# Multiplying w2 and the first 16 rows of wo in three TensorE loops with register addresses

## The chip, the cores and the metric

The kernel runs on one NeuronCore of a Trainium2 chip. The metric is the device time of one execution in microseconds. The core has five engines with instruction streams of their own: TensorE (PE; its weight loads are listed apart as PEld), VectorE (DVE), ScalarE (ACT), GpSimd (POOL) and SyncE (SP), which here only issues transfers. Each engine has a sequencer that reads the instructions, runs branches, register work and waits itself, and hands the rest to the engine. Data moves between HBM and the on-chip memory (SBUF, 128 partitions) through 16 DMA engines; TensorE writes its results to another memory, PSUM.

## What is computed

One decoded token `x` (1,024 values) is normalised, and two branches are added to it: attention with 32 query heads over the last 4,096 positions of a cache with 4 key/value heads, and a two-layer MLP.

```python
xn = _layernorm(x)
# A: attention over the last W = 4096 positions
q = xn @ wq                                   # 32 heads x 128
p = softmax(q . k / sqrt(128))                # k, v repeated 8 times
o = p . v                                     # 4096 values
A = o @ wo                                    # [4096] x [4096, 1024]
# B: MLP
h = gelu(layernorm(xn) @ w1 + b1)             # 3584 values
B = h @ w2 + b2                               # [3584] x [3584, 1024]
out = x + A + B
```

All tensors are bfloat16. Nearly all of the work is reading 39.9 MB: 4 MB each of K and V, and the matrices wq, w1, w2 and wo.

## The kernel before

With one token, every product is a vector times a matrix. The vector is the stationary operand of TensorE, one column of 128 values at a time, and the matrix streams through in pieces of 128 rows by 512 columns; the result is one row of 512 sums in PSUM. To use more of the array, such matmuls are placed in groups of columns of the array that start at 0, 32, 64 or 96 (`tile_position`); the output row then lies in the PSUM partition of the same number.

The stages follow each other so. The large transfers go through one queue that SP issues: K (L72), wq (L81), w1 (L207), V (L213), w2 (L221), wo (L229). They land in a ring of four tiles of 32 KB per partition, so a transfer waits until an older tile of the ring has been read. w2 comes in two tiles of 14 rows each, wo in two tiles of 16 rows; a "row" here is a piece of 128 matrix rows by 1,024 columns. The second wo tile is transferred in five parts, of 8, 4, 2, 1 and 1 rows, so that the last part to land is small.

Meanwhile VectorE and ScalarE transpose K (L186 to L202), TensorE forms q (L238) and the first MLP layer (L258), the scores (L276), the softmax follows, and TensorE multiplies the probabilities with V (L320). The first MLP layer's sums pass through the gelu on ScalarE (L313) and a transpose on VectorE (L315) into `hT`, whose column 32c holds the 128 values of h that belong to row c of w2. The attention result is brought into the same form as `o8` (L330 to L332), one column of 128 values per row of wo.

The last stage adds everything up in the PSUM tile `accf`, whose partitions 0 and 32 hold the two halves of the 1,024 outputs; x and b2 have been put there early (L178). A loop in the kernel's Python, unrolled into straight code (L339 to L342), goes over the 28 rows of w2 and 28 of the 32 rows of wo. Each row takes two matmuls, one for each half: the first in the column group at 0, the second in the group at 32. The last four rows of wo are the tail: their sums go to two other PSUM tiles, while ScalarE and VectorE copy `accf` out (L345, L346); the two parts are added (L353, L361, L362) and written to HBM.

POOL clears and fills small constants at the start, and computes the two reciprocal roots of the layer norms (L145, L168).

Of the kernel before, what the change touches and what calls it, by code (L numbers as in the profile page):

```python
# [9 lines left out]
BF16 = mybir.dt.bfloat16  # L10
# [6 lines left out]
def kernel(  # L17
# [14 lines left out]
    nc = tc.nc  # L32
    P = 128
    D = A_x.shape[-1]
# [12 lines left out]
    CW2 = Fd // P  # L47
    CWO = NQ // P
# [5 lines left out]
    consts = ctx.enter_context(tc.tile_pool(name="consts", bufs=1))  # L54
# [8 lines left out]
    def ring_tile(name):  # L63
        return ring.tile([P, RING_ELEMS], BF16, tag="ring", name=name, align_bytes=256)
# [13 lines left out]
    for i in range(2):  # L78
        t = ring_tile(f"wq{i}")
# [92 lines left out]
    accf = ps_acc.tile([P, 512], FP32, tag="accf")  # L172
# [3 lines left out]
    for half in range(2):  # L176
        pr = 32 * half
        nc.tensor.matmul(accf[pr:pr + 1, :], lhsT=ones_bf[0:2, 0:1], rhs=xb2[:, 512 * half:512 * half + 512],  # L178
                         start=True, stop=False, tile_position=(0, pr))
# [24 lines left out]
    for i in range(2):  # L204
        t = ring_tile(f"w1{i}")
# [6 lines left out]
        src = A_v_cache[0, g0:g1, Sk - W:Sk, :].rearrange("g (p c) d -> p g c d", p=P)  # L212
        nc.sync.dma_start(out=v4[:, g0:g1, :, :], in_=src)  # L213

    chunk_src = []
    w2_v = B_w2.rearrange("(p c) n -> p c n", p=P)
    for i in range(2):
        nr = CW2 // 2
        t = ring_tile(f"w2{i}")
        tv = t[:, :nr * D].rearrange("p (r n) -> p r n", r=nr)  # L220
        nc.sync.dma_start(out=tv, in_=w2_v[:, nr * i:nr * (i + 1), :])  # L221
        chunk_src += [("h", nr * i + r, tv[:, r, :]) for r in range(nr)]
    wo_v = A_wo.rearrange("(p c) n -> p c n", p=P)
    for i, cuts in enumerate([[0, 16], [0, 8, 12, 14, 15, 16]]):
        nr = CWO // 2
        t = ring_tile(f"wo{i}")
        tv = t[:].rearrange("p (r n) -> p r n", r=nr)
        for a, b in zip(cuts[:-1], cuts[1:]):
            nc.sync.dma_start(out=tv[:, a:b, :], in_=wo_v[:, nr * i + a:nr * i + b, :])  # L229
        chunk_src += [("o", nr * i + r, tv[:, r, :]) for r in range(nr)]  # L230


    for i, w3 in enumerate(wq_tiles):
        for r in range(4):
            c = 4 * i + r
            for j in range(NJQ):
                b, t = divmod(j, 4)
                nc.tensor.matmul(accq[32 * t:32 * t + 1, b, :], lhsT=xnT[:, c:c + 1], rhs=w3[:, r, j * 512:(j + 1) * 512],  # L238
                                 start=(c == 0), stop=(c == C - 1), tile_position=(0, 32 * t))
# [8 lines left out]
    for j in range(8):  # L248
        t, b = divmod(j, 2)
        nc.tensor.matmul(acch[32 * t:32 * t + 1, b, :NH], lhsT=ones_bf[0:1, 0:1], rhs=b1_row[:, j * NH:(j + 1) * NH],  # L250
                         start=True, stop=False, tile_position=(0, 32 * t))
    for i, w3 in enumerate(w1_tiles):
        for r in range(4):
            c = 4 * i + r
            for b in range(2):
                for t in range(4):
                    j = 2 * t + b
                    nc.tensor.matmul(acch[32 * t:32 * t + 1, b, :NH], lhsT=yT[:, c:c + 1], rhs=w3[:, r, j * NH:(j + 1) * NH],  # L258
                                     start=False, stop=(c == C - 1), tile_position=(0, 32 * t))
# [11 lines left out]
    for a in range(WQ4 // 512):  # L271
        sp = ps_f.tile([P, 512], FP32, tag="pf", name="sp")
        for R in range(4):
            for g in range(Hkv):
                c0 = WQ4 * R + 512 * a
                nc.tensor.matmul(sp[32 * R:32 * R + 32, :], lhsT=qm[:, g, :], rhs=kT[:, g, c0:c0 + 512],  # L276
                                 start=(g == 0), stop=(g == Hkv - 1), tile_position=(0, 32 * R))
# [31 lines left out]
    h_sb = consts.tile([P, 2 * NH], BF16)  # L309
    zcol = small.tile([P, 1], FP32, tag="zcol")  # L310
    nc.vector.tensor_scalar_mul(out=zcol[:], in0=l_loc[:], scalar1=0.0)  # L311
    for b in range(2):
        nc.scalar.activation(out=h_sb[:, b * NH:(b + 1) * NH], in_=acch[:, b, :NH], func=ACT.Gelu_apprx_tanh, bias=zcol[:])  # L313
    hT = consts.tile([P, CW2, 32], BF16)
    nc.vector.transpose(out=hT[:], in_=h_sb[:].rearrange("p (d c) -> p c d", c=CW2))  # L315


    o_all = ps_f.tile([Hq, Hkv, Dh], FP32, tag="pf", name="o_all")
    for c in range(NCH):
        nc.tensor.matmul(o_all[:].rearrange("h g d -> h (g d)"), lhsT=eTb[:, 32 * c:32 * c + 32], rhs=v4[:, :, c, :],  # L320
                         start=(c == 0), stop=(c == NCH - 1))
# [6 lines left out]
    o8_ps = ps_f.tile([P, 32], FP32, tag="pf", name="o8_ps")  # L328
    for q in range(4):
        nc.tensor.matmul(o8_ps[:], lhsT=spread[:, q, :], rhs=o_bf[:, 32 * q:32 * q + 32], start=(q == 0), stop=(q == 3))  # L330
    o8 = consts.tile([P, 32], BF16)
    nc.vector.tensor_copy(out=o8[:], in_=o8_ps[:])  # L332


    vec = {"h": lambda c: hT[:, c, 0:1], "o": lambda c: o8[:, c:c + 1]}
    N1 = 320
    TAIL = 4
    n_bulk = len(chunk_src) - TAIL
    for idx, (kind, c, wap) in enumerate(chunk_src[:n_bulk]):  # L339
        for half in range(2):  # L340
            nc.tensor.matmul(accf[32 * half:32 * half + 1, :], lhsT=vec[kind](c), rhs=wap[:, half * 512:(half + 1) * 512],  # L341
                             start=False, stop=(idx == n_bulk - 1), tile_position=(0, 32 * half))  # L342
# [7 lines left out]
    for idx, (kind, c, wap) in enumerate(chunk_src[n_bulk:]):  # L350
        if idx == TAIL - 2:
            for half in range(2):
                nc.tensor.matmul(acct[1][32 * half:32 * half + 1, :], lhsT=ident_f[0:33, 32 * half:32 * half + 1], rhs=bulk[1][:],  # L353
                                 start=False, stop=False, tile_position=(0, 32 * half))
        for t, (n0, n1) in zip(acct, cols):
            for half in range(2):
                nc.tensor.matmul(t[32 * half:32 * half + 1, :], lhsT=vec[kind](c),  # L357
                                 rhs=wap[:, half * 512 + n0:half * 512 + n1],
                                 start=(idx == 0), stop=(idx == TAIL - 1), tile_position=(0, 32 * half))
# [36 lines left out]
```

## Time and profile before

| | us |
|---|---|
| runs, median of 2 (101.69 to 102.08) | 101.88 |
| span of the profiled execution | 100.0 |
| median over the profiled span | 1.9 |
| PE busy / PEld busy | 51.2 / 20.0 |
| DVE busy / ACT busy / POOL busy | 49.7 / 34.1 / 3.8 |
| mean granted TensorE clock | 0.778 of full speed |
| read from HBM | 39.86 MB, 398 GB/s over the span |

The span runs from the first to the last instruction of one execution that the hardware profiler recorded; the 1.9 us beside it lie around the program. A busy time is the time in which an engine has at least one instruction under way. Waits, branches, register work and the issuing of transfers are not counted as busy. The granted clock is the share of TensorE's full clock that it was given, which changes during the run between 0.5 and 1. In all tables of the profile L12 is line 12 of the kernel, `out<-in` names the tiles, and "<-" behind an idle time names what ended it.

### The profile page before, as it was taken

Reading aid. Unit: us, or ns where it says so; the run is one execution under the profiler, and the core shown is the slowest. Engines: PE = TensorE matmul, PEld = TensorE weight load, DVE = VectorE, ACT = ScalarE, POOL = GpSimd, SP = SyncE. Lnnn points to the kernel's source line nnn. Section 1 sums busy time; section 2 is a strip of 40 time slices with the busy share of each in tenths; the row PEclk is TensorE's granted clock in tenths of the full one; section 3 lists DMA queues with packets and bytes.
Section 4 is the critical chain, followed back from the end, with each engine's and each line's share of the span. In section 5 each row is a group of like instructions: output and inputs, shape, how many; then the busy total and the mean of one; then the engine's idle time right before and its main releaser. Section 6 shows DMA issues by size and latency. Waiting matters only on the chain.

```text
span 100.0 us, 970 instructions
## 1 busy us (share of the span) xinstructions
PE 51.2 (51%) x365; PEld 20.0 (20%) x365; DVE 49.7 (50%) x92; ACT 34.1 (34%) x37; POOL 3.8 (4%) x16
## 2 busy tenths in 40 slices
PE   0065200008500940193892935999469950199980
PEld 0042200002100310031530322334123410033320
DVE  5445499999999999997125115410450000000021
ACT  5000002999999999962001044400000000000010
POOL 6005200000000000000000000000000000000000
PEclk9999999999995579555555555559985998557999
DMA  2999999999999999998999999999999999999920
GB/s 26 394 420 426 491 488 472 419 419 419 432 419 393 401 500 382 413 482 378 390 429 426 429 531 390 413 477 390 459 447 426 419 432 419 406 419 411 401 73 1
DMA packets 2878, 39.92 MB, mean 399 GB/s; under 512 B 309, under 2 KB 311, under 8 KB 698
## 3 DMA queue, kind: packets, MB, share of 16 engines
q1 hardware_dynamic: 2866, 39.85, 93.6%
q8 instruction: 3, 0.05, 0.2%
q10 hardware_dynamic: 8, 0.01, 0.0%
q14 instruction: 1, 0.01, 0.0%
HBM read 39.86 MB, written 0.00 MB: 398 GB/s over the span
## 4 chain that ended last, share of the span: by engine, by line
DVE 38%; DMA 24%; PE 21%; issue 9%; POOL 3%; ACT 2%; SPq 1%; POOLq 1%; ACTq 0%
DMA wo<-in_A_wo_dram 24%; DVE kt_scr L186 17%; DVE kT L202 16%; PE o_all L320 10%; PE sp L276 4%; PE acch L258 3%; ACT e L298 1%; DVE eTb L300 1%; PE qT_ps L262 1%; DVE m_loc L284 1%; PE acct L357 1%; SPq L229 1%; DVE q_sb L241 1%; POOLq L391 1%; POOL spread L110 1%
## 5 line engine op out<-in xcount | busy, mean ns | idle before, releaser
L200 ACT COPY kT<-kt_scr 32x1024 bf16<-32x1024 bf16 x26 | 27.1, 1042 | 14.8 <-DVE kt_scr L186 14.5
L186 DVE STREAM_TRANSPOSE kt_scr<-k_sb 128x4096 bf16<-128x4096 bf16 x4 | 17.4, 4411 | 0.0
L238 PE MATMUL accq<-wq,xnT 128*1 128x512 bf16 x64 | 7.1, 622 | 18.3 <-DMA wq<-in_A_wq_dram 18.3
L202 DVE COPY kT<-kt_scr 32x1024 bf16<-32x1024 bf16 x38 | 15.9, 419 | 0.5
L346 DVE COPY bulk<-accf 33x320 f32<-33x320 f32 x1 | 0.5, 483 | 21.9 <-ACT bulk L345 21.9
L341 PE MATMUL accf<-wo,o 128*1 128x512 bf16 x56 | 8.3, 459 | 6.0 <-DMA wo<-in_A_wo_dram 5.9
L345 ACT COPY bulk<-accf 33x192 f32<-33x192 f32 x1 | 0.3, 312 | 31.9 <-PE accf L341 31.9
L320 PE MATMUL o_all<-v_sb,eTb 128*32 128x512 bf16 x32 | 10.0, 491 | 1.0 <-DVE zcol L311 1.0
L258 PE MATMUL acch<-w,yT 128*1 128x448 bf16 x64 | 6.3, 572 | 6.0 <-DMA w<-in_B_w_dram 6.0
L341 PE MATMUL accf<-w,hT 128*1 128x512 bf16 x56 | 7.9, 451 | 0.0
L238 PEld LDWEIGHTS <-xnT 128*1 128x1 bf16 x64 | 2.1, 116 | 22.5 <-issue 22.4
L320 PEld LDWEIGHTS <-eTb 128*32 128x32 bf16 x32 | 3.8, 120 | 6.9 <-issue 3.9
L341 PEld LDWEIGHTS <-o 128*1 128x1 bf16 x56 | 2.8, 97 | 11.4 <-issue 9.2
L258 PEld LDWEIGHTS <-yT 128*1 128x1 bf16 x64 | 2.0, 115 | 9.8 <-issue 9.8
L276 PE MATMUL sp<-kT,qm 128*32 128x512 bf16 x32 | 3.8, 630 | 0.3 <-DVE qm L267 0.3
L341 PEld LDWEIGHTS <-hT 128*1 128x1 bf16 x56 | 2.7, 96 | 4.7 <-issue 2.5
L323 DVE TENSOR_TENSOR o_m<-o_all,grs 32x512 f32<-32x512 f32 x1 | 0.7, 680 | 5.8 <-PE o_all L320 5.8
L123 PE MATMUL x_ps<-ones_bf,xb 1*128 1x1 bf16 x8 | 0.7, 200 | 5.0 <-DMA xb<-in_A_x_dram 5.0
L298 ACT ACTIVATE e<-sc,nmx 128x1024 bf16<-128x1024 f32 x1 | 1.1, 1148 | 5.7 <-DVE nmx L295 5.7
L315 DVE STREAM_TRANSPOSE hT<-h_sb 128x896 bf16<-128x896 bf16 x1 | 1.7, 1706 | 2.4 <-ACT h_sb L313 2.4
L276 PEld LDWEIGHTS <-qm 128*32 128x32 bf16 x32 | 2.1, 133 | 1.4 <-issue 0.9
L281 ACT COPY sc<-sp 128x512 f32<-128x512 f32 x1 | 0.6, 585 | 4.8 <-PE sp L276 4.8
(88 smaller groups left out, 35.9 us busy)
## 6 DMA issues: line engine op xcount, KB each, us to landing
w<-in_B_w_dram SPq DMA_DIRECT2D x4, 3584.0 KB
wq<-in_A_wq_dram SPq DMA_DIRECT2D x2, 4096.0 KB, 27.0
k_sb<-in_A_k_cache_dram SPq DMA_DIRECT2D x4, 1024.0 KB, 7.1
wo<-in_A_wo_dram SPq DMA_DIRECT2D x1, 4096.0 KB, 29.4
v_sb<-in_A_v_cache_dram SPq DMA_DIRECT2D x1, 2048.0 KB, 19.2
v_sb<-in_A_v_cache_dram SPq DMA_DIRECT2D x2, 1024.0 KB, 23.1
wo<-in_A_wo_dram SPq DMA_DIRECT2D x1, 2048.0 KB
wo<-in_A_wo_dram SPq DMA_DIRECT2D x1, 1024.0 KB
```

The source lines that it names most:

```text
L110: nc.gpsimd.affine_select(out=spread[:], in_=spread[:], compare_op=ALU.not_equal, fill=1.0, base=0, pattern=[[-1, 4], [1, P]], channel_mul ...
L186: nc.vector.transpose(out=scr[:, g, :], in_=k2[:, g, :])
L200: nc.scalar.copy(out=dst, in_=src)
L202: nc.vector.tensor_copy(out=dst, in_=src)
L229: nc.sync.dma_start(out=tv[:, a:b, :], in_=wo_v[:, nr * i + a:nr * i + b, :])
L238: nc.tensor.matmul(accq[32 * t:32 * t + 1, b, :], lhsT=xnT[:, c:c + 1], rhs=w3[:, r, j * 512:(j + 1) * 512], start=(c == 0), stop=(c == C ...
L258: nc.tensor.matmul(acch[32 * t:32 * t + 1, b, :NH], lhsT=yT[:, c:c + 1], rhs=w3[:, r, j * NH:(j + 1) * NH], start=False, stop=(c == C - 1) ...
L276: nc.tensor.matmul(sp[32 * R:32 * R + 32, :], lhsT=qm[:, g, :], rhs=kT[:, g, c0:c0 + 512], start=(g == 0), stop=(g == Hkv - 1), tile_posit ...
L298: nc.scalar.activation(out=e128[:], in_=sc[:], func=ACT.Exp, bias=nmx[:], scale=scale, accum_out=l_loc[:])
L315: nc.vector.transpose(out=hT[:], in_=h_sb[:].rearrange("p (d c) -> p c d", c=CW2))
L320: nc.tensor.matmul(o_all[:].rearrange("h g d -> h (g d)"), lhsT=eTb[:, 32 * c:32 * c + 32], rhs=v4[:, :, c, :], start=(c == 0), stop=(c == ...
L341: nc.tensor.matmul(accf[32 * half:32 * half + 1, :], lhsT=vec[kind](c), rhs=wap[:, half * 512:(half + 1) * 512], start=False, stop=(idx == ...
```

## The change

The straight code for the 28 rows of w2 and the first 16 rows of wo becomes three loops that TensorE runs itself, one for each of the first three tiles of the last stage. The 12 rows of the second wo tile that belong to the bulk, and the tail, stay straight code.

A loop's body handles two rows with four matmuls. The place of the stationary columns and of the matrix piece in SBUF is worked out from the loop's counter in registers. For this the columns of h and o stand 64 apart in larger tiles that POOL has cleared, with zeros between them. A matmul loads 64 columns of which one holds values and 63 are zero: starting 32 columns ahead of the values for the second half, at the values for the first. So the values' row of sums falls in partition 32 or 0, and every matmul writes partitions 0 to 63 of `accf`, adding zeros to all but one.

Each loop stands in a critical section, a block of its own in the program that the scheduler does not mix with other instructions.

```diff
     for i in range(2):
         nr = CW2 // 2
         t = ring_tile(f"w2{i}")
...
+        bulk_tiles.append(t)
...
-    hT = consts.tile([P, CW2, 32], BF16)
-    nc.vector.transpose(out=hT[:], in_=h_sb[:].rearrange("p (d c) -> p c d", c=CW2))
+    hT = consts.tile([P, 64 * CW2 + 64], BF16)
+    nc.gpsimd.memset(hT[:], 0.0)
+    nc.vector.transpose(out=hT[:, 32:32 + 64 * CW2].rearrange("p (c f) -> p c f", f=64)[:, :, 0:32],
+                        in_=h_sb[:].rearrange("p (d c) -> p c d", c=CW2))
...
-    o8 = consts.tile([P, 32], BF16)
-    nc.vector.tensor_copy(out=o8[:], in_=o8_ps[:])
+    o8 = consts.tile([P, 64 * CWO + 64], BF16)
+    nc.gpsimd.memset(o8[:], 0.0)
+    nc.vector.tensor_copy(out=o8[:, 32:32 + 64 * CWO:64], in_=o8_ps[:])
...
-    vec = {"h": lambda c: hT[:, c, 0:1], "o": lambda c: o8[:, c:c + 1]}
+    vec = {"h": lambda c: hT[:, 32 + 64 * c:33 + 64 * c], "o": lambda c: o8[:, 32 + 64 * c:33 + 64 * c]}
...
-    for idx, (kind, c, wap) in enumerate(chunk_src[:n_bulk]):
+    def rows_in_loop(z, c0, w_tile, n, unroll):
+        with tc.tile_critical(sync_engine=mybir.EngineType.PE):
+            with nc.tensor.Fori(0, n // unroll) as i:
+                for u in range(unroll):
+                    for half in range(2):
+                        nc.tensor.matmul(accf[0:64, :], lhsT=z[:, bass.ds((i * unroll + u) * 64 + 64 * c0 + 32 - 32 * half, 64)],
+                                         rhs=w_tile[:, bass.ds((i * unroll + u) * D + half * 512, 512)],
+                                         start=False, stop=False, skip_group_check=True)
+
+    rows_in_loop(hT, 0, bulk_tiles[0], CW2 // 2, 2)
+    rows_in_loop(hT, CW2 // 2, bulk_tiles[1], CW2 // 2, 2)
+    rows_in_loop(o8, 0, bulk_tiles[2], CWO // 2, 2)
+    for idx, (kind, c, wap) in list(enumerate(chunk_src[:n_bulk]))[CW2 + CWO // 2:]:
```

## The prediction

> **What bounds the kernel now.** The page's slices come first. Columns are 2.5 us each; the digits are tenths busy, granted clock and mean DMA share.
>
> ```profile
> PE   0065200008500940193892935999469950199980
> PEclk9999999999995579555555555559985998557999
> DMA  2999999999999999998999999999999999999920
> ```
>
> The DMA row is 9 from the second slice to the 38th: the inputs stream without a break, and TensorE idles between bursts. The chain that ended last says the same of the end; its columns are start, us and what.
>
> ```profile
> 61.20 10.05 PE o_all L320 x32
> ...
> 72.11 23.63 DMA wo<-in_A_wo_dram
> ...
> 95.79 0.60 PE acct L357 x8
> ```
>
> So the end waits for the last rows of wo. How closely TensorE follows is in its timeline:
>
> ```profile
> 61.20 10.04 PE L320 MATMUL o_all<-v_sb,eTb 128*32 128x512 bf16 x32 [1.02 <-DVE zcol L311]
> 73.30 0.25 PE L330 MATMUL o_ps<-o_bf,spread 32*128 32x32 bf16 x4 [2.06 <-DVE o_bf L327]
> 73.47 7.89 PE L341 MATMUL accf<-w,hT 128*1 128x512 bf16 x56
> 87.27 8.31 PE L341 MATMUL accf<-wo,o 128*1 128x512 bf16 x56 [5.91 <-DMA wo<-in_A_wo_dram]
> ```
>
> All of w2 is multiplied by 81.36, then TensorE idles 5.91 us until the first wo tile is there (87.27), and the last bulk matmul ends at 87.27 + 8.31 = 95.58, just before the tail's rows. TensorE has 5.9 us to spare before 87.3 and almost none behind it.
>
> What a matmul costs is in the busy time by stretches (us, then PE's busy time and count, its weight loads, granted clock, DMA share). The first two lines are L320's matmuls alone, one column group; the last two are L341's, which alternate between two column groups.
>
> ```profile
> 63.80:67.20 3.40, 3.40 (x10) 1.19 (x9) 0.50 1.08 460
> 67.20:70.60 3.40, 3.40 (x17) 1.54 (x16) 1.00 1.04 447
> ...
> 74.05:77.46 3.41, 3.41 (x20) 1.06 (x16) 0.50 1.04 447
> 77.46:80.87 3.41, 3.41 (x34) 1.41 (x32) 1.00 1.04 452
> ```
>
> With one or two at each border taken off, L320 makes 16 matmuls in 3.40 us at full clock, 0.213 us each, and 8 at half clock, 0.427 us each; its weight loads are hidden. L341 makes 32 and 16: two column groups at once, so a row's two halves cost 0.213 us together, 0.427 at half clock.
>
> **The array's price.** The change writes both halves to one group of 64 columns, so its matmuls have L320's pace: a row costs 0.427 us at full clock and 0.853 at half, twice the old price. An iteration of two rows takes 0.85 or 1.71 us; there are 7 + 7 + 8 = 22.
>
> **The sequencer's price.** The built program shows what an iteration is for TensorE's sequencer: six fused register instructions holding 27 register operations, one more addition, a compare-and-branch, four matmuls (each a weight load and a matmul) whose addresses come from registers. No row of before is a loop. The nearest rows, from L320's own view, the start of the chain of waits (start, us, what) and TensorE's timeline: a wait on TensorE's sequencer, 51 ns; POOL's register move, 0.03 us; 0.10 us ahead of POOL's first work, which holds that engine's branch into the kernel; and the eight tiny matmuls of L123, paced by issue and loading alone.
>
> ```profile
> L320 PEldq EVENT_SEMAPHORE  x1: 51/51/51, 60.4 to 60.4; - x1
> ...
> 0.69 0.10 issue
> ...
> 8.46 0.03 POOLq L110
> ...
> 4.96 0.66 PE L123 MATMUL x_ps<-ones_bf,xb 1*128 1x1 bf16 x8 [4.96 <-DMA xb<-in_A_x_dram]
> ```
>
> L123: (0.66 - 0.20 for the last one) / 7 = 0.066 us a pair. Lower end: seven register instructions at 0.03, four pairs at 0.066, a branch at 0.05: 0.52 us. Upper end: 28 operations at 51 ns, eight loads and matmuls at 0.10, a branch at 0.10: 2.33. I take 28 x 0.03 = 0.84 (fused or not, the operations follow each other), 8 x 0.066 = 0.53 (a register address doubles the price of a pair) and 0.10: 1.47 us.
>
> A page has a price for the branch: the Trainium skill, "Advanced Engine Details and Errata", section Control Flow Timing, gives about 108 ns for a compare-and-branch. By that figure the sum would be 0.2 us longer over all iterations; no run here shows one.
>
> At half clock the array (1.71) is then slower than the sequencer (1.47), so it is busy throughout and the clock rises, as after 74.05:77.46; at full clock it is busy 0.85 / 1.47 = 58% of the time. Stretches from 46.7 to 63.8 with TensorE busy 47 to 81% all stood at 0.50, and after 70.6:74.05, 40% busy, the clock fell. So I expect it to change back and forth, and an iteration of (1.71 + 1.47) / 2 = 1.6 us.
>
> **The waits the change adds.** A loop stands in a section of its own, and the built program puts waits on TensorE's sequencer before each: for every transfer issued ahead of it in the program, not only for its own tile. The first loop waits for both w2 tiles, the second for the first wo tile, the third for the second wo tile's first 8 rows. In the trace they landed at 76.1, 87.2 and 92.1 us. Behind these waits stands everything left on TensorE; nobody else waits, since the DMA issues of wo ask only for L258 and L320, which stay ahead. So the first loop starts 2.6 us later than L341 did, and the second cannot use the old idle time before 87.2. Entry after the wait: two branches, a move and the wait itself, 0.3 us. Between loops the array drains (about 0.2), some ten waits at 51 ns and three branches: 1.0 us, between 0.5 and 1.5. Leaving the third: 0.5.
>
> **Edits priced at nothing.** POOL clears 1,856 columns for hT between its two rstd steps (L145 ends at 9.05, L168 starts at 11.53). By its memsets of 128 and 512 columns (0.19 and 0.51 us) a column costs 0.83 ns: 1.6 us. The idle time there is 1.45 us and one mask of 0.2 us moves behind L168, so that step slips by 0 to 0.3 us, and with it yT and VectorE's transposes. The 2,112 columns for o8 (1.8 us) run beside the first transpose, at 0 to 1.8 us if the two get in each other's way. Either slip is covered by the 2.6 us for which the first loop waits for w2; without that cover it would cost its full size. The transpose L315 writes its 32-column blocks apart: 1.7 us, 1.7 to 3.4, ended at 65.5 and not needed before 76. The o8 copy (0.19) has two loops to hide in. SP passes a branch before its wo issues and waits for nothing new; a later issue of 0.1 us is hidden by the backlog (wo takes 29.4 us from issue to landing). The DMA stream keeps its end, 97 us.
>
> **The sum.** First matmul 76.1 + 0.3 = 76.4; loops 22 x 1.6 = 35.2; two passages 2.0; exit 0.5; the 12 straight rows of wo left, 8 at half clock and 4 at full, 4.3. The bulk ends at 118.4 instead of 95.58: 22.8 us later. All transfers are long done then; the tail behind the bulk took 97.4 - 95.58 = 1.8 us and is set by the same copy, matmuls and addition. Span 100.0 + 22.8 = 122.8; the runs' median stands 1.9 us above the profiled span, for what lies around it: 124.7 us.
>
> **The rivals.**
> Fast loops: the sequencer's price is at its lower end and the array runs at full clock where it can. The first loop ends near 84.6, the second still waits for 87.2, starts cold (two iterations at 1.71, five at 0.85) and ends at 95.4; 0.5, then 8 x 0.85 = 6.8, then 0.3 + 2.6: 105.6, 10.0 later, 111.9 us. For it: register work is light and TensorE queues ahead. Against: every gapped stretch above stood at half clock.
> Slow sequencer: 2.33 us an iteration: 76.4 + 51.3 + 3.0 + 0.5 + 5.1 = 136.3, 142.6 us. For it: TensorE's wait takes 51 ns where POOL's move takes 30.
> Code loading: the jump back fetches its code anew each time. The page's third part has the price:
>
> ```profile
> q8 instruction: 3, 0.05, 0.2%
> ```
>
> 0.2% of 16 engines over 100 us is 3.2 us for three blocks, 1.07 us each; 19 jumps back cost 20 us more: 145. Against: an iteration is 16 instructions. The Trainium skill, "Runtime: NRT & Kernel Launch", section Instruction fetch mechanics, has a taken branch stall for a fetch only when its target lies outside the pages held; by that rule the loops stay inside and only their entries could stall. No run here shows it.
> Not slower: the entry waits do not hold (loops start when their own tile is there) and the array runs at full clock, at 0.85 us an iteration. The 5.91 us of idle time before 87.27 then swallow both w2 loops; behind it 6.8 + 0.3 + 2.6 = 9.7 replace 8.31: 103.3 us. It decides at 0.92 us an iteration or less; above, the change is slower by over 2%. Against: the program has the waits, and the clock was 0.50 until 91.1. That straight code runs instead of loops is excluded by the built program.
>
> **How the numbers follow.** Chances: the forecast's case, 1.25 to 2.1 us an iteration (117 to 137 us), 0.62; fast loops 0.13; slow sequencer 0.11; code loading 0.10; not slower 0.04, of which 0.01 for a gain. The range goes from the fast loops, 112, to the slow sequencer, 143. Two per cent, 2.0 us, is about what a measurement of this kernel tells from no change: faster 0.01, same 0.03, slower 0.96.
>
> **What would show it.** The first loop's matmul starting near 76.4, not 73.5; the second's not before 87.2. Matmuls of one loop 0.427 us apart at clock 0.50, never two together. An iteration of four every 1.6 us; gaps without a releaser would be the sequencer's. The landings of wo near 97 as before. If the loops' stretch lasts under 25 us or over 50, my sequencer price is wrong; if wo lands later, so is the claim that the stream is untouched.

## The result, and the profile after

The changed kernel takes 117.04 us in the median (117.03 to 117.05), beside 101.88 before: 1.149 times as long, with a 95% interval from 1.144 to 1.154. Its profiled span is 115.3 us. The forecast was 124.7, its range 112 to 143. Ratios, here and below, compare fast runs alone: a run over 1.5% above the fastest of its kernel counts as slow, as two of the four runs of one experiment below and three of the four of another do.

The slices of the changed kernel, 2.9 us to a column now:

```profile
PE   0261200092064037184846996009994996788890
PEclk9999999999999755958755599655599679999999
DMA  3999999898899989899999999989899990000000
```

The DMA row ends seven columns before the span does: the stream stopped where it stopped before (wo's last part landed at 96.8 instead of 97.0), and the rest is TensorE alone. Its timeline, with start, duration, tiles, count and the idle time ahead:

```profile
72.99 0.26 PE L334 MATMUL o_ps<-o_bf,spread 32*128 32x32 bf16 x4 [2.06 <-DVE o_bf L331]
78.05 8.82 PE L349 MATMUL accf<-w,hT 128*64 x28 [4.80 <-DMA w<-in_B_w_dram]
88.56 1.05 PE L349 MATMUL accf<-w,hT 128*64 x4 [1.69 <-issue]
89.81 7.08 PE L349 MATMUL accf<-w,hT 128*64 x24 [0.20 <-issue]
98.69 2.23 PE L349 MATMUL accf<-wo,o 128*64 x8 [1.80 <-issue]
101.08 1.05 PE L349 MATMUL accf<-wo,o 128*64 x4 [0.16 <-issue]
102.28 1.04 PE L349 MATMUL accf<-wo,o 128*64 x4 [0.15 <-issue]
103.50 2.23 PE L349 MATMUL accf<-wo,o 128*64 x8 [0.18 <-issue]
...
108.51 2.75 PE L358 MATMUL accf<-wo,o 128*1 128x512 bf16 x24 [0.38 <-PEq L345]
```

The first loop does not start when its own tile and h are ready (its tile landed at 68.9) but after 4.80 us of idle time: its section waits for w2's second tile as well (77.35). The second starts 1.69 us after the first has ended, behind wo's first tile (landed at 87.0). In the third every four matmuls start 1.20 to 1.22 us after the four before, with a gap that ends in nothing but "issue": there the sequencer sets the pace. The bulk ends at 108.51 + 2.75 = 111.26 instead of 95.58, 15.7 us later. All of it arises behind 87 us. Before, TensorE had 8.31 us of work left there. Now it has 1.6 up to the second loop's start, a second w2 loop of 8.3, a passage of 1.8, the third loop of 9.4, an exit of 0.4 and the last rows, 2.75: 24.3 us.

The sequencer's rows, by the two source lines of a loop (durations in ns, minimum, median and maximum):

```profile
L349 PEldq FUSED_REGOPS  x110: 42/64/84, 77.9 to 107.5; - x110
...
L346 PEldq FUSED_REGOPS  x22: 78/78/83, 77.8 to 106.8; - x22
L346 PEldq ALU_OP  x22: 36/36/39, 78.6 to 107.7; - x22
L346 PEldq COMPARE_BRANCH  x22: 76/213/237, 78.8 to 107.8; - x22
```

An iteration holds five fused instructions of 64 ns in the median, one of 78, an addition of 36 and a branch of 213: 0.65 us. The other 0.55 us of the 1.20 go to the eight loads and matmuls and to the steps between the 16 instructions. The sequencer keeps this pace where the array is slower, too. In the first loop, at half clock, its branches start at 78.8, 80.0, 81.2 and 82.4 us, 1.2 us apart, while groups of four matmuls start 1.71 us apart; at full clock the array then catches up, with groups 0.86 us apart.

### The profile page after: what moved, and what is told of

Read it like the earlier page. It is cut to its first block, busy times and chain, and to the rows that moved or that the text cites. A ratio compares the mean times of both kernels' runs of the same rounds, so it can differ in the third digit from the quotient of the medians.

```text
span 115.3 us, 1194 instructions
## 1 busy us (share of the span) xinstructions
PE 60.8 (53%) x365; PEld 25.8 (22%) x365; DVE 51.2 (44%) x92; ACT 34.1 (30%) x37; POOL 7.1 (6%) x18
## 3 DMA queue, kind: packets, MB, share of 16 engines
q1 hardware_dynamic: 2866, 39.85, 81.2%
## 5 line engine op out<-in xcount | busy, mean ns | idle before, releaser
L349 PE MATMUL accf<-w,hT 128*64 x56 | 17.0, 473 | 6.7 <-DMA w<-in_B_w_dram 4.8
L349 PEld LDWEIGHTS accf<-w,hT 128*64 x56 | 7.4, 133 | 15.9 <-issue 12.9
L324 PE MATMUL o_all<-v_sb,eTb 128*32 128x512 bf16 x32 | 9.4, 467 | 1.0 <-DVE zcol L313 1.0
L349 PE MATMUL accf<-wo,o 128*64 x32 | 8.4, 384 | 2.9 <-issue 2.6
L260 PE MATMUL acch<-w,yT 128*1 128x448 bf16 x64 | 5.8, 537 | 6.3 <-DMA w<-in_B_w_dram 6.3
L349 PEld LDWEIGHTS accf<-wo,o 128*64 x32 | 3.4, 106 | 7.8 <-issue 7.0
L278 PE MATMUL sp<-kT,qm 128*32 128x512 bf16 x32 | 3.3, 570 | 0.4 <-DVE qm L269 0.4
L358 PE MATMUL accf<-wo,o 128*1 128x512 bf16 x24 | 2.8, 379 | 0.4 <-PEq L345 0.4
L264 PE MATMUL qT_ps<-ident,q_sb 128*128 128x128 bf16 x8 | 0.9, 240 | 3.2 <-DVE q_sb L243 3.0
```

The lines of the kernel that those rows point to most:

```text
L349: nc.tensor.matmul(accf[0:64, :], lhsT=z[:, bass.ds((i * unroll + u) * 64 + 64 * c0 + 32 - 32 * half, 64)], rhs=w_tile[:, bass.ds((i * unr ...
```

## The experiments

Three explanations stood against each other. Wait theory: the loops cost what the sequencer takes, plus the entries, whose waits push the second w2 loop behind wo's landing. Array theory: the cost is one column group where there were two. Share theory: each loop costs its share of the iterations, wherever it stands.

**The same matmuls without loops.** All 44 rows use the 64-column matmuls between the zeros, as straight code.

```diff
-        with tc.tile_critical(sync_engine=mybir.EngineType.PE):
-            with nc.tensor.Fori(0, n // unroll) as i:
...
+        for r in range(n):
+            for half in range(2):
+                a = 64 * (c0 + r) + 32 - 32 * half
+                nc.tensor.matmul(accf[0:64, :], lhsT=z[:, a:a + 64], rhs=w_tile[:, r * D + half * 512:r * D + half * 512 + 512],
+                                 start=False, stop=False, skip_group_check=True)
```

> The same 64-column matmuls between the same zeros, as straight code: no loops, no sections. Sequencer theory (what the loops cost is their sequencer's pace and their entries): the array alone at one matmul per 0.213 us (0.427 at half clock) starts near 73.4, takes w2 to about 87.5 and thus keeps the clock, ends the bulk near 97 and costs about 1 us: 102.9 us, between 102.0 and 104.5. Array theory (one column group instead of two is the cost): within 2 us of the changed kernel's 117. The cleared tiles stay in, so a late VectorE chain would show here too.

Measured: 102.91 us, 1.010 times before (1.008 to 1.013). TensorE's timeline:

```profile
72.46 13.83 PE L348 MATMUL accf<-w,hT 128*64 128x512 bf16 x56
87.12 7.07 PE L348 MATMUL accf<-wo,o 128*64 128x512 bf16 x32 [0.83 <-DMA wo<-in_A_wo_dram]
94.12 2.75 PE L356 MATMUL accf<-wo,o 128*1 128x512 bf16 x24
```

w2 takes 13.83 us instead of 7.89 and fills the idle time before 87.1. Before took 101.99 us beside it, so the lost column group costs 0.9 us of 15.2; array theory falls.

**A quarter of the columns in the loops.** The instructions stay, each matmul streams 128 columns; three quarters of the product in these rows is left out.

```diff
-                        nc.tensor.matmul(accf[0:64, :], lhsT=z[:, bass.ds((i * unroll + u) * 64 + 64 * c0 + 32 - 32 * half, 64)],
-                                         rhs=w_tile[:, bass.ds((i * unroll + u) * D + half * 512, 512)],
+                        nc.tensor.matmul(accf[0:64, 0:128], lhsT=z[:, bass.ds((i * unroll + u) * 64 + 64 * c0 + 32 - 32 * half, 64)],
+                                         rhs=w_tile[:, bass.ds((i * unroll + u) * D + half * 512, 128)],
```

> In the loops each matmul streams 128 columns instead of 512, so three quarters of these rows' product is left out; the loops' instructions stay the same. Sequencer theory: an iteration still takes 1.2 us in all three loops, and the time stays at 117 or goes up to 119.6, since the lighter array may leave the clock at half for the straight rows behind. Array theory: the array needs 0.43 us an iteration at half clock, loops end some 9 us earlier, 108 us.

Measured: 118.88 us, ratio to before 1.166 (1.161 to 1.171). Iterations of the first loop, and the straight rows behind the loops:

```profile
79.68 0.87 PE L349 MATMUL accf<-w,hT 128*64 x4 [0.42 <-issue]
80.88 0.89 PE L349 MATMUL accf<-w,hT 128*64 x4 [0.32 <-issue]
82.09 0.86 PE L349 MATMUL accf<-w,hT 128*64 x4 [0.32 <-issue]
...
108.23 4.92 PE L358 MATMUL accf<-wo,o 128*1 128x512 bf16 x24 [0.42 <-PEq L345]
```

With a quarter of the array's work an iteration still takes 1.20 us, at half clock throughout. So 1.2 us is the sequencer's own price: a lighter array does not lower it. The kernel is slower still because the straight rows now run at half clock: 4.92 us instead of 2.75.

**Longer bodies.** Seven, seven and eight rows in a body instead of two.

```diff
-    rows_in_loop(hT, 0, bulk_tiles[0], CW2 // 2, 2)
-    rows_in_loop(hT, CW2 // 2, bulk_tiles[1], CW2 // 2, 2)
-    rows_in_loop(o8, 0, bulk_tiles[2], CWO // 2, 2)
+    rows_in_loop(hT, 0, bulk_tiles[0], CW2 // 2, 7)
+    rows_in_loop(hT, CW2 // 2, bulk_tiles[1], CW2 // 2, 7)
+    rows_in_loop(o8, 0, bulk_tiles[2], CWO // 2, 8)
```

> Two iterations a loop instead of 7, 7 and 8: seven or eight rows in a body. Sequencer theory: without most branches the sequencer needs about 0.42 us a row (from 1.205 us less 0.37 for addition, branch and restart, over two rows), just under the array's 0.432 at full clock, so rows come every 0.43 us at full clock: loop 3 takes 6.9 instead of 9.4 us, loop 2 up to 1.8 less, 112.3 to 113.9 us. Array theory: nothing changes, 117.

Measured: 113.40 us (112.65 to 114.13), ratio to before 1.110 (1.104 to 1.117).

```profile
88.23 7.89 PE L349 MATMUL accf<-w,hT 128*64 x28 [2.21 <-issue]
97.88 7.29 PE L349 MATMUL accf<-wo,o 128*64 x32 [1.76 <-DMA wo<-in_A_wo_dram]
```

The third loop takes 7.3 us instead of 9.4, against 6.9 expected: 0.456 us a row. The sequencer's first branch back there starts 3.66 us before its last one, with eight rows between them, 0.457 us a row instead of the 0.42 expected. So it still sets the pace, just above the array's 0.43. The short bodies, with their additions, branches and restarts, cost 3.6 us of the whole. In this profile the first loop ended at 86.02 and wo's first tile landed at 87.14, so the second section's wait lengthened the passage, 2.21 us instead of 1.69.

**Each section waits for its own tile.** In the changed kernel a section's entry waits for every transfer that stands ahead of it in the program. Here each later transfer stands behind the loop of the tile before; a fence holds the scheduler to that order and waits for nothing.

```diff
...
     rows_in_loop(hT, 0, bulk_tiles[0], CW2 // 2, 2)
+    tc.no_sync_barrier()
+    load_w2(1)
     rows_in_loop(hT, CW2 // 2, bulk_tiles[1], CW2 // 2, 2)
+    tc.no_sync_barrier()
+    load_wo(0, [0, 16])
     rows_in_loop(o8, 0, bulk_tiles[2], CWO // 2, 2)
+    tc.no_sync_barrier()
+    load_wo(1, [0, 8, 12, 14, 15, 16])
...
```

> The transfers of the second w2 tile and of wo stand behind the loop of the tile before in the program, so each section waits only for its own tile (SP passes sections without waiting, the transfers are issued as before). Wait theory: the first loop starts near 73.9 instead of 78.05, the second does not wait for wo, loops end 3 to 4 us earlier: 113.4 us (112.5 to 114.5). If the waits only move time about (the clock, or wo's landing sets the third loop's start): 116 to 117.

Measured: 111.77, 113.13, 115.47 and 115.82 us; the ratio, by the first two, is 1.104 (1.095 to 1.112). The profiled run is the one of 115.47.

```profile
74.55 0.25 PE L338 MATMUL o_ps<-o_bf,spread 32*128 32x32 bf16 x4 [2.06 <-DVE o_bf L335]
76.18 9.10 PE L352 MATMUL accf<-w,hT 128*64 x28 [1.39 <-DMA w<-in_B_w_dram]
86.97 1.05 PE L352 MATMUL accf<-w,hT 128*64 x4 [1.69 <-DMA wo<-in_A_wo_dram]
```

The first two runs are 5.3 and 3.9 us below the changed kernel, one in the bounds expected and one under them; the other two are only 1.6 and 1.2 below, above the bounds. The start near 73.9 was missed in this profile: the attention result came late (74.55 instead of 72.99), and the entry takes 1.4 us behind it although w2's first tile had landed at 69.0. The first loop still starts 1.9 us earlier than in the changed kernel. The releasers that these lines name had nothing to do with the waits: wo's first tile landed only at 87.14, after the second loop had started.

The passages remain, 1.69 and 1.80 us, as long as in the changed kernel. So there the second section's wait for wo cost nothing: the first loop ended at 86.87, and the passage alone leads to 88.56. What the waits cost the changed kernel is the late start of the first loop. Why these four runs lie 4 us apart is not shown. In the profiles of all kernels here the attention result (`o_ps`) starts between 71.5 and 74.8 us; a wait for w2's second tile hides such a difference, and here nothing does. But only one run of this kernel was profiled.

**One section for all three loops.** It lengthens the suspected wait.

```diff
-        with tc.tile_critical(sync_engine=mybir.EngineType.PE):
...
+    with tc.tile_critical(sync_engine=mybir.EngineType.PE):
+        rows_in_loop(hT, 0, bulk_tiles[0], CW2 // 2, 2)
+        rows_in_loop(hT, CW2 // 2, bulk_tiles[1], CW2 // 2, 2)
+        rows_in_loop(o8, 0, bulk_tiles[2], CWO // 2, 2)
```

> All three loops in one section. Wait theory: its entry waits for the first 8 rows of the second wo tile (91.9), the first loop starts near 92.7, at half clock at first, and no passages between sections are left: the bulk ends near 124.8, 130.6 us (129 to 132). If the entry waits cost little beside the loops: 115 to 117, a little under the changed kernel, for the two passages saved.

Measured: 128.63 us, ratio 1.263 (1.260 to 1.266); 0.4 us below the lower bound given.

```profile
93.32 11.96 PE L348 MATMUL accf<-w,hT 128*64 x40 [18.29 <-DMA wo<-in_A_wo_dram]
```

w2 has been there since 77.6, yet its first matmul waits 18.29 us for a part of wo that it does not read (landed at 92.1). The entry waits are real.

**One kind of loop at a time.** First only wo's 16 rows in a loop, then only w2's 28; the other rows are straight code with two column groups.

```diff
-    rows_in_loop(hT, 0, bulk_tiles[0], CW2 // 2, 2)
-    rows_in_loop(hT, CW2 // 2, bulk_tiles[1], CW2 // 2, 2)
...
+    rows_straight(0, CW2)
     rows_in_loop(o8, 0, bulk_tiles[2], CWO // 2, 2)
```

> w2 as before in straight code, one loop for the 16 rows of wo. Wait theory: the section's entry waits for the first part of the second wo tile, at 91.9 instead of 87.1; eight iterations from 92.6 on, the first two or three at half clock; the bulk ends near 106.4: 112.1 us (111 to 113.5). Share theory (each loop costs by its iterations, 8 of 22 of 15.2 us): 107.4.

```diff
     rows_in_loop(hT, 0, bulk_tiles[0], CW2 // 2, 2)
     rows_in_loop(hT, CW2 // 2, bulk_tiles[1], CW2 // 2, 2)
-    rows_in_loop(o8, 0, bulk_tiles[2], CWO // 2, 2)
+    rows_straight(CW2, CW2 + CWO // 2)
```

> The two w2 loops stay, the 16 rows of wo are straight code as before. Wait theory: the second loop waits for wo's first tile and ends near 96.9 as in the changed kernel; then 28 straight rows at 0.213 us, bulk end 103.4: 109.2 us (108 to 110.5). Share theory (14 of 22 iterations of 15.2 us): 111.6.

Measured: 111.92 us (ratio 1.097 to 1.103) and 109.59 us (1.069 to 1.082). wo's loop alone, 8 iterations of 22, costs more than both w2 loops, 14 of 22; share theory falls. The reason is in the first one's timeline:

```profile
77.67 4.87 PE L356 MATMUL accf<-w,hT 128*1 128x512 bf16 x28 [2.80 <-DMA w<-in_B_w_dram]
93.33 9.63 PE L349 MATMUL accf<-wo,o 128*64 x32 [10.78 <-DMA wo<-in_A_wo_dram]
```

The loop starts 6 us after its own tile has landed (87.3), because its section waits for the next one (92.1).

**The wide layout alone.** Cleared tiles and columns 64 apart, all rows straight as before.

```diff
-    rows_in_loop(hT, 0, bulk_tiles[0], CW2 // 2, 2)
-    rows_in_loop(hT, CW2 // 2, bulk_tiles[1], CW2 // 2, 2)
-    rows_in_loop(o8, 0, bulk_tiles[2], CWO // 2, 2)
-    for idx, (kind, c, wap) in list(enumerate(chunk_src[:n_bulk]))[CW2 + CWO // 2:]:
+    for idx, (kind, c, wap) in enumerate(chunk_src[:n_bulk]):
```

> The cleared, wider tiles for h and o alone; all rows in straight code as before, one column and two column groups. Cover theory: GpSimd's clearing holds up VectorE's step beside it and VectorE's transposes start about 1.4 us later, as in the changed kernel, but the stream of transfers hides it: 101.9 us, within 0.5. If the delay reaches the end: 103.3.

Measured: 101.74 us, ratio 0.999 (0.997 to 1.000). VectorE's transposes start at 13.57 instead of 12.32, and nothing of it reaches the end.

**A loop where there is cover.** Only the first w2 tile, with the wait for its own tile; all else straight.

```diff
...
     rows_in_loop(hT, 0, bulk_tiles[0], CW2 // 2, 2)
-    rows_in_loop(hT, CW2 // 2, bulk_tiles[1], CW2 // 2, 2)
-    rows_in_loop(o8, 0, bulk_tiles[2], CWO // 2, 2)
-    for idx, (kind, c, wap) in list(enumerate(chunk_src[:n_bulk]))[CW2 + CWO // 2:]:
+    tc.no_sync_barrier()
+    load_w2(1)
+    load_wo(0, [0, 16])
+    load_wo(1, [0, 8, 12, 14, 15, 16])
...
+    for idx, (kind, c, wap) in list(enumerate(chunk_src[:n_bulk]))[CW2 // 2:]:
```

> One loop for the first w2 tile, waiting for its own tile alone; all other rows straight as before. Cover theory: the loop starts between 74 and 76.2, takes about 9 us and ends near 85; 14 rows of w2 at 0.213 us follow until 88.7 and 16 of wo until 92.2, so TensorE has caught up with the stream (94.4) before its last parts land: 102.0 us (101.5 to 103). Share theory (7 of 22 iterations of 15.2 us): 106.7.

Measured: 101.99 us, ratio 1.001 (0.999 to 1.002).

```profile
76.17 9.15 PE L352 MATMUL accf<-w,hT 128*64 x28 [1.30 <-DMA w<-in_B_w_dram]
85.51 3.19 PE L364 MATMUL accf<-w,hT 128*1 128x512 bf16 x28 [0.19 <-PEq L348]
88.52 5.37 PE L364 MATMUL accf<-wo,o 128*1 128x512 bf16 x48
94.45 1.03 PE L364 MATMUL accf<-wo,o 128*1 128x512 bf16 x8 [0.56 <-DMA wo<-in_A_wo_dram]
```

A loop as slow as the changed kernel's own first one costs nothing: TensorE has caught up by 93.9 and waits for wo again. What counts is what is left behind 87 us.

**Own waits and longer bodies together.** The edits of "Longer bodies" and of "Each section waits for its own tile" in one kernel.

> Both remedies together: each section waits for its own tile alone, and seven, seven and eight rows to a body. If the two gains add up (2.7 and 3.6 us of 117.0): 110.7. By the parts: first loop from 76.2 to 85.1, 1.7 between loops, 6.1, 1.8, 6.9, then 0.4 and 2.75: the bulk ends near 104.8, 110.5 us (109.5 to 112.5). It stays slower than before, since two loops' rows and passages lie behind the first wo tile.

Measured: 107.23, 110.00, 111.21 and 111.32 us, the median 110.61; before took 101.93 beside it. The profiled run is the one of 111.21:

```profile
76.03 9.10 PE L352 MATMUL accf<-w,hT 128*64 x28 [1.39 <-DMA w<-in_B_w_dram]
86.78 6.50 PE L352 MATMUL accf<-w,hT 128*64 x28 [1.65 <-DMA wo<-in_A_wo_dram]
95.08 7.26 PE L352 MATMUL accf<-wo,o 128*64 x32 [1.79 <-DMA wo<-in_A_wo_dram]
```

The parts came about as forecast: the bulk ends at 105.43 in this run, against 104.8. Whether the two gains add up is not shown. The 2.7 us taken for the own waits are the median of runs that lie 4 us apart; by the two lowest of them the sum would be 4.6 + 3.6 = 8.2 us, and the lowest run here is 9.8 below the changed kernel, the others 5.7 to 7.0. Between 5.3 and 9.4 us remain over the kernel before: the second w2 loop starts only at 86.78, and the passage behind it lies behind wo's landing, too. No kernel with all three loops came nearer than this lowest run, 5% above the kernel before.

## Why the prediction was right, and where its sizes were off

**The bound.** Right: the stream kept its end, and TensorE, which had almost nothing to spare behind 87 us, became the bound.

**The entry waits.** Right for the first loop: it started at 78.05, behind w2's second tile, and the experiments show this wait by lengthening it (one section) and taking it away (own waits). The forecast start was 76.4. The landing of w2's second tile, given as 76.1 us, was misread: that is an update halfway through the sixteen that make up a landing. The last one came at 77.35 (77.56 before the change). The entry itself took 0.7 us, not 0.3. The second loop started at 88.56, behind wo's landing, but not because of its wait: the first loop ended at 86.87, and the passage took the rest. In the forecast's own sum, too, only the first wait costs anything.

**The array's price.** Right: 0.427 us a matmul at half clock, 0.213 at full, one at a time. Here is the clock through the loops (stretch, length, TensorE's busy time and count, granted clock, DMA share):

```profile
79.93:83.34 3.41, 3.41 (x10) 0.50 1.07 461
83.34:86.76 3.42, 3.42 (x17) 1.00 0.89 383
86.76:90.17 3.41, 1.52 (x7) 1.00 0.97 413
90.17:93.58 3.41, 3.41 (x10) 0.50 0.98 410
93.58:96.99 3.41, 3.31 (x15) 1.00 0.53 205
...
100.41:103.82 3.41, 2.92 (x13) 1.00 0.00 0
```

Eight matmuls to a stretch at half clock (less the overlaps at the borders), up to 16 at full.

**The iteration.** This is the term that was mis-sized: 1.6 us forecast. The sequencer takes 1.20 instead of 1.47. I priced the 28 register operations one by one, at 0.84 us; fused, they take about 0.43 with the addition. The branch was too cheap at 0.10: it takes 0.21. The 0.10 us ahead of POOL's first work, from which it was taken, was a gap; the trace of before has no row of a branch. The loads and matmuls, with the steps between all instructions, came out as taken, 0.55 beside 0.53.

Two more things were wrong in the way from these prices to 1.6. An iteration was to take 1.71 us whenever the array was at half clock. But the sequencer ran on at 1.20 meanwhile, and the array made up for its lag at full clock, with two rows every 0.86 us. And the clock does not go back and forth at every other stretch. It stood at half from 73.1 to 83.34, through the long wait and the first stretches behind it, and fell again behind a passage (86.76:90.17, busy 45% of the stretch), but the third loop, with an array that works 0.85 of 1.20 us, kept full clock to the end. The mean over 22 iterations is (8.8 + 8.3 + 9.4) / 22 = 1.21 us, just outside the 1.25 to 2.1 us that the forecast's case was to cover.

The page of the Trainium skill that I named, "Advanced Engine Details and Errata", section Control Flow Timing, gives 108 ns for a compare-and-branch; the trace shows 213 ns for one that jumps back and 76 for one that falls through, so the trace decides.

**The sum.** That the second loop's start was right (88.6) was luck: the first loop began 1.65 us late, was 2.4 shorter, and the passage behind it 0.7 longer. From there: 2.9 us less in the second loop, 3.4 less in the third, 1.5 less for the 12 straight rows at full clock, 0.8 more in the passage (1.8 instead of 1.0), 0.1 less at the exit. That is 7.1 us, the distance from 118.4 to 111.26. The tail took 1.4 instead of 1.8.

**The edits priced at nothing.** The verdict holds (the layout alone: 101.74 us), the way there does not. I expected a slip of 0 to 0.3 us from the order on POOL. The profiles show another mechanism. The first line is the kernel before, the others are the changed one:

```profile
9.09 0.60 DVE L146 TENSOR_SCALAR xn_f<-xc,rstd 128x8 f32<-128x8 f32 x1 [0.40 <-POOL rstd L145]
...
9.09 1.65 POOL L317 MEMSET hT<- 128x1856 bf16 x1
9.17 1.59 DVE L146 TENSOR_SCALAR xn_f<-xc,rstd 128x8 f32<-128x8 f32 x1 [0.41 <-POOL rstd L145]
```

VectorE's small step beside the clearing took 1.59 us instead of 0.60 and ended with it; the transposes began at 13.78 instead of 12.32. The cover that was named for it, the first loop's wait for w2, was there. The Trainium skill, "Advanced Engine Details and Errata", section VectorE Performance Modes, says that VectorE's second port to SBUF is shared with GpSimd and that the two can block each other. The trace agrees in that this step waited for the clearing's end; it does not show by which port. The transposes beside the second clearing kept their time (4.44 us before and after).

**The rivals.** Fast loops would have given 111.9. The result lies between them and the forecast, since the sequencer's price does, too. Code loading is excluded: the jump back takes 0.21 us, and the profile's page lists two blocks of instructions instead of three. The slow sequencer is excluded by the 1.20 us. "Not slower" named the right cover: one loop inside it costs nothing (101.99 us). Three do not fit: even with own waits the second started at 86.97.

## What to carry to other kernels

A loop on an engine's sequencer has a price of its own, here 1.2 us for two rows, with the whole of the array's work or a quarter of it, so it is free only under a wait that is longer. Before putting code in a section that the scheduler treats as one piece, list what its entry waits for: here it waited for tiles that it did not read, up to 18 us in the worst arrangement. And count what is left behind the last landing, not the work as a whole: a loop of 7 iterations cost nothing ahead of it, and one of 8 behind it cost 10 us, its wait included.

## What the runs showed of the hardware

- A passage from one loop's section to the next takes 1.7 to 1.8 us on TensorE between the last and the first matmul, with every awaited transfer landed: eight or nine semaphore instructions of 51 ns and two no-ops of 13 ns, a little over 0.1 us apart, a drain, and a branch of 174 ns into the section.
- In these runs the clock changed only at borders 3.41 us apart. It rose behind stretches that TensorE's rows filled (79.93:83.34) or filled to 91% (longer bodies, 77.97:81.38), and did not rise behind stretches filled to 71 to 77% (the loops with a quarter of the columns). It fell behind a stretch busy for 1.52 us (45%), and in another run behind one of 1.56 us; behind 1.58 us it was kept once (after the second passage) and fell once (the first loop alone, 95.76:99.18). So near there the busy time of one stretch does not settle it.
- The loops with a quarter of the columns left the clock at half from 75 to 113 us, and the straight code behind it paid for that with 2.2 us.
